# Gated linear attention with a maxout layer: a new order of the first loads, other due times in the planner, and two copies moved between engines

## The chip, the cores and the metric

The kernel runs on one core of one Trainium2 chip. The metric is the device time of one execution in microseconds (us). The core has five engines with a queue each: TensorE (PE), VectorE (DVE), ScalarE (ACT), GpSimd (POOL) and SyncE (SP), which here only issues loads. Each engine runs its instructions in the order of its program and waits at an instruction until what it needs is there.

## The reference: what is computed

```python
# q, k, v, alpha: (4 batches, 8 heads, 768 tokens, 48)
for t in range(S):
    state = alpha[:, :, t, :, None] * state + einsum('bhd,bhe->bhde', k[:, :, t], v[:, :, t])
    y[:, :, t] = einsum('bhd,bhde->bhe', q[:, :, t], state)
x = y.transpose(0, 2, 1, 3).reshape(3072, 384)
h1 = x @ w1                      # 384 x 1024
h2 = x @ w2                      # 384 x 1024
out = maximum(h1, h2) @ w_out    # 1024 x 384
```

## The kernel before

**Algebra.** The maxout is rewritten: max(h1, h2) = relu(x (w1 - w2)) + x w2. So the kernel forms `w12` = w1 - w2 (DVE, L447) and `w2o` = w2 w_out, and each output is relu(x w12) w_out + x w2o. The recurrence is done in chunks of 128 tokens: the logarithms of alpha are summed along the chunk, k is divided and q multiplied by the exponentials of the sums, and inside a chunk everything is a matmul.

**Units.** The 24 chunks go in pairs, so there are 12 units u = 0 to 11; unit u is batch u % 4 and token range u // 4. For a unit `gla(u)` makes: the logarithm of alpha on ACT (L468), the sums on PE (L490 for units 0 to 2, L479 after), the exponentials on ACT (`em` L517, in place in PSUM L519, `de` L522), `kn` on POOL (L560), `qn` on DVE (L562), their transposes on PE (L570) and the copy out of PSUM on DVE (`qu` L573 for units 0 to 2, `qk` L578 after), k by v on PE (`kv`, L589 or L632), the state `tm` (DVE L644; for the first chunk of a batch a plain copy, on ACT at L646 while u < TM_ACT, else on DVE at L648) and the scaled state `sb` on POOL (L619), q by k on PE (L661), the masked copy `pt` of it on DVE (four of them in a unit, L683), y on PE (L692, L695), and x transposed: `yc` on ACT (L703), PE L709, `xt` on DVE (L714 or L718). Then `moe(u)`: four groups `hp` on PE (L749, six matmuls each) with a relu into `gt` on ACT (L760) or DVE (L757), and the output sums on PE (L780: three matmuls with `w2o`, eight with `wo16`), a copy on ACT (L788) and the store.

**Weights.** w2 comes in three blocks of 512 KB (here w20, w21, w22), w_out in four of 384 KB (wo0 to wo3), w1 in four of 384 KB (w10 to w13). A w2 block goes through a cast on ACT (`w2h` L420), eight transposes on PE (L427), a copy out of PSUM (`w2T` L431, on ACT if its number is in WT_ACT, else on DVE) and eight matmuls with `wo16` (L437). `wo16` is the cast of w_out: block 0 on ACT, 1 to 3 on POOL (L452). Group g of `hp` needs `w12` group g, thus w1 block g and all three blocks of w2.

**Order.** Nothing is ordered by hand. Every step goes to a planner with `add`: engine, estimated duration, what it reads and writes, a key, and a `lat`, the time from its end to its result's being of use. `schedule` (L69) plays the steps in its own model of time: whenever an engine is free it takes, of the steps whose inputs have arrived in the model, the one with the smallest key. The instructions are then written in the order of the planned starts. So the planner's times set only the order; on the chip each engine waits for what is really late. Keys: 10 u plus a small number for `gla(u)`, 10 u + 20 (KEY_M) plus a small number for `moe(u)`, 3 (KEY_W) for the casts, transposes and copies of the weights, 11 (KEY_W12) for `w12`, 12 (KEY_WO) for the matmuls and copies of `w2o`. Eight PSUM banks are shared under CAPS.

**Loads.** All loads are issued by SP. The first 19 follow the list HEAD: a0 is alpha of unit 0, k1 is k of unit 1, and so on, each 384 KB for units 0 and 1. Their place on SP is fixed by the list. `load` and `load_w` give the planner their landing: SP's time for the issue plus a `lat` of 2.5 us (3.1 for w2), more for later units through LATE and LATER.

**Fillers.** Where the plan leaves PE idle in the first 40 us, matmuls on a constant are written in (L458); they produce nothing.

The lines that the change and the steps touch are in `load` (L382), `load_w` (L409), `w2_rows` (L419), `Plan.add` (L43, where PRI shifts a key) and the loop over HEAD (L816).

Of the kernel before, what the change touches and what calls it, by code (L numbers as in the profile page):

```python
# [23 lines left out]
class Plan:  # L24
# [18 lines left out]
    def add(self, eng, fn, dur, reads=(), writes=(), key=0.0, lat=None, ps=(), tiled=False, join=None):  # L43
        if writes:
            x = writes[0] if isinstance(writes[0], tuple) else writes
            d = self.pri.get(f"{eng}:{'.'.join(str(y) for y in x)}@{self.u}", 0)
            key, join = key + d, None if join is None else join + d
        o = Op(len(self.ops), eng, fn, dur, self.LAT[eng] + self.PAD if lat is None else lat, key)
        o.tiled, o.join = tiled, key if join is None else join
        for r in reads:  # L50
            if r in self.last_w:
                o.deps.add(self.last_w[r])
            self.readers.setdefault(r, []).append(o.n)
        for w in writes:
            if w in self.last_w:
                o.deps.add(self.last_w[w])
            for r in self.readers.pop(w, ()):
                if r != o.n:
                    o.deps.add(r)
            self.last_w[w] = o.n  # L60
        for x in (*reads, *writes, *ps):
            if x in self.psum and x not in o.ps:
                o.ps.append(x)
                self.psum[x][2] += 1
        o.w = (*writes, *reads)[:1]
        self.ops.append(o)
        return o
# [118 lines left out]

KEY_W12 = 11
KEY_W = 3
KEY_WO = 12
KEY_M = 20  # L190
CAPS = {'g': 6, 'm': 5, 'w': 3}
W12_POOL = ()
WT_ACT = ()
WO_ACT = (0,)
RELU_DVE = 1
TM_ACT = 1
X_LAST = 0
LATER = 0.6
LATE = 2.5
KEY_T2 = 17  # L200
TWO = (0, 1, 2)
# [7 lines left out]
PAIR_ON = 'POOL'  # L209
KN_DVE = ()  # L210
VX_DVE = ()
PRI = {}
HEAD = 'k0 a0 a1 q0 v0 k1 q1 w20 w22 w21 wo0 v1 wo1 wo2 wo3 w11 w10 w13 w12'


@with_exitstack
def kernel(
# [18 lines left out]
    nc = tc.nc  # L236
# [10 lines left out]
    def sbt(name, shape, dt, n=1):  # L247
        return [constp.tile(shape, dt, name=f"{name}{i}") for i in range(n)]
# [26 lines left out]
    w2h, = sbt("w2h", [128, ND, DFF], FP16)  # L275
    w12, = sbt("w12", [128, ND, DFF], FP16)
# [12 lines left out]
    def nat(t):  # L289
        return t.rearrange("p (a h d) -> p a h d", a=2, h=H)  # L290
# [4 lines left out]
    P = Plan()  # L295
    P.pri, P.u = PRI, None
    add = P.add
# [4 lines left out]
    def b32(x, n):  # L302
        return bank(x)[:, 0:n]
# [75 lines left out]
        add("DVE", lambda i=i: nc.vector.memset(SB[i], 0.0), 0.2, writes=[("sb", i)], key=-4)  # L379


    def load(u, what="akqv"):  # L382
        n, (b, cp) = u % NLD, (u % B, u // B)
        t0 = 256 * cp
        lat = 2.5 + max(0.0, min(LATE, LATE * (u - 1) / 3.0)) + LATER * max(0, u - 4)
        ws = [({4: "w2f", 5: "w1f", 6: "wof"}[u], g) for g in range(3 if u == 4 else 4)] if u in (4, 5, 6) else []

        def pairs(dst, src, keys):
            add("SP", lambda: nc.sync.dma_start(  # L389
                out=dst.rearrange("p (h x) -> p h x", h=H),  # L390
                in_=src[b, :, t0 : t0 + 256, :].rearrange("h (p r) d -> p h (r d)", r=2)),
                1.26 if u in TWO else 1.5, writes=[*keys, *ws], key=-1, lat=lat)

        if "a" in what:
            pairs(LD[n][:, 0, :], alpha, [("af", n)])
        rest = [x for x in (("k", "kf", KF, k), ("q", "qf", QF, q), ("v", "vf", VF, v)) if x[0] in what]
        if u in TWO:
            for _, nm, T, src in rest:
                pairs(T[n], src, [(nm, n, 0), (nm, n, 1)])
            return  # L400
        for a in range(2):
            for _, nm, T, src in rest:
                add("SP", lambda T=T, src=src, a=a: nc.sync.dma_start(
                    out=nat(T[n])[:, a],
                    in_=src[b, :, t0 + 128 * a : t0 + 128 * a + 128, :].rearrange("h p d -> p h d")),
                    0.99, writes=[(nm, n, a), *ws], key=-1, lat=lat)


    def load_w(m, g):  # L409
        fs = slice(256 * g, 256 * g + 256)  # L410
        if m == "2":
            dst, src, t = w2f[:, g, :], moe_w2[128 * g : 128 * g + 128, :], 1.36
        elif m == "1":
            dst, src, t = w1f[:, :, fs], moe_w1[:, fs].rearrange("(s p) f -> p s f", p=128), 1.15
        else:
            dst, src, t = wof[:, 2 * g : 2 * g + 2, :], moe_w_out[fs, :].rearrange("(s p) d -> p s d", p=128), 1.1
        add("SP", lambda: nc.sync.dma_start(out=dst, in_=src), t, writes=[(f"w{m}f", g)], key=-1, lat=3.1 if m == "2" else 2.5)

    def w2_rows(ds):  # L419
        add("ACT", lambda: nc.scalar.copy(out=w2h[:, ds, :], in_=w2f[:, ds, :]),  # L420
# [7 lines left out]
        add("PE", w_t, 0.445, reads=[("w2h", ds), "ident"], writes=[x], key=KEY_W)  # L428
        on = ds in WT_ACT
        cp = nc.scalar.copy if on else nc.vector.tensor_copy  # L430
# [5 lines left out]
        for f in range(NF):  # L436
            add("PE", lambda f=f: nc.tensor.matmul(  # L437
                b32(y, DM), lhsT=w2T[:, f, 128 * ds : 128 * ds + 128], rhs=wo16[:, f, :],
                start=(f == 0), stop=(f == NF - 1)),
                0.162, reads=[("w2T", ds), ("wo16", f // 2)], writes=[y], key=KEY_WO)  # L440
        add("ACT", lambda: nc.scalar.copy(out=w2o[:, ds, :], in_=b32(y, DM)),
            0.38, reads=[y], writes=[("w2o", ds)], key=KEY_WO)

# [81 lines left out]
    def gla(u):  # L525
# [69 lines left out]
        def chunk(a):  # L595
# [27 lines left out]
            if more:  # L623
# [14 lines left out]
                for h2 in range(2):  # L638
                    r, e = slice(64 * h2, 64 * h2 + 64), slice(D * h2, D * h2 + D)

                    def e_tm(r=r, e=e):
                        t = b32(kvp, DM).rearrange("p (j w) -> p j w", j=HP)
                        if has:
                            nc.vector.tensor_add(out=TM[tmi][r], in0=t[r, :, e], in1=sb[r, :, e])  # L644
                        elif u < TM_ACT:
                            nc.scalar.copy(out=TM[tmi][r], in_=t[r, :, e])  # L646
                        else:
                            nc.vector.tensor_copy(out=TM[tmi][r], in_=t[r, :, e])  # L648
                    on_act = not has and u < TM_ACT
                    add("ACT" if on_act else "DVE", e_tm, 0.32 if on_act else 0.37, reads=[kvp] + ([("sb", m4, h2)] if has else []),  # L650
# [162 lines left out]
    for ds in range(ND):  # L813
        P.ps(f"wq{ds}", 1, "w")
    add("SP", lambda: None, 0.6, key=-3)
    for x in HEAD.split():  # L816
        if x[0] == "w":
            load_w(x[1], int(x[2]))
        else:
            load(int(x[1]), x[0])  # L820
    gla(0)
    for g in range(4):
        weights(g)
# [2 lines left out]
    for u in range(NU):  # L826
        if u + 1 < NU:
            if f"a{u + 1}" not in HEAD:
                load(u + 1)
            gla(u + 1)  # L830
        moe(u)
# [38 lines left out]
```

## Time and profile before

| what | us |
|---|---|
| median of 5 runs | 138.8 (138.65 to 139.34) |
| the profiled execution, its own time | 138.8 |
| its span, first to last instruction | 137.1 |
| what lies around the span | 1.7 |
| PE busy, fillers (L458) among it | 130.6, of them 10.1 |
| DVE, ACT, POOL busy | 95.7, 81.8, 74.9 |
| first `hp` matmul of unit 0 starts | 25.38 |
| load queue of SP, share of the 16 DMA engines over the span | 71.7% |

The clock that PE was granted is full in all forty slices of the page. The page gives PE as 95% busy, but matmuls on the filler constant count as busy, so PE's row alone does not tell how much of the first 25 us is work; the table by stages and the filler rows do. A load's landing is its issue time plus the time to landing of its row. The times to the left in a timeline count from the start of the span.

### The profile page before, as it was taken

To read this page: it belongs to the slowest core of one execution; us is meant where nothing else is said; L and a number is where in the kernel's file an instruction comes from. 1 tells how busy PE (TensorE), PEld (TensorE's weight loads), DVE (VectorE), ACT (ScalarE), POOL (GpSimd) and SP (SyncE) were. 2 spreads that over 40 slices of the span, in tenths; PEclk is the share of its full clock that TensorE was granted. 3 is DMA by queue.
4 is the path that set the end of the run, shared out by engine and by line. 5 is a ranking of instruction groups with operands and counts; after the bars stand their busy time and mean duration, and the time that the engine had idled before them with its cause. 6 is when DMAs were issued, how large, how long until landed. Compare 5 with 4: busy or idle time off the path is not lost.

```text
span 137.1 us, 4253 instructions
## 1 busy us (share of the span) xinstructions
PE 130.6 (95%) x1671; PEld 101.4 (74%) x1671; DVE 95.7 (70%) x204; ACT 81.8 (60%) x174; POOL 74.9 (55%) x138
## 2 busy tenths in 40 slices
PE   6897999999999999999999999999999999999990
PEld 6776975777868777777877877777777778777870
DVE  4965999943799985966958859849839568583300
ACT  3394890879875765853944845837738548244440
POOL 7467549028596296574763972864757839200000
PEclk9999999999999999999999999999999999999999
DMA  4999999999997999979999999989978030030202
GB/s 98 324 325 402 374 374 352 289 251 254 260 268 153 271 223 195 299 149 213 286 183 306 230 223 260 236 176 271 258 140 225 5 115 2 5 115 0 105 29 100
DMA packets 84180, 28.59 MB, mean 209 GB/s; under 512 B 78400, under 2 KB 83392, under 8 KB 84160
## 3 DMA queue, kind: packets, MB, share of 16 engines
q1 hardware_dynamic: 81120, 23.60, 71.7%
q10 hardware_dynamic: 3040, 4.72, 9.1%
q8 instruction: 13, 0.21, 0.6%
q14 instruction: 7, 0.06, 0.1%
HBM read 23.59 MB, written 4.72 MB: 207 GB/s over the span
## 4 chain that ended last, share of the span: by engine, by line
PE 84%; DMA 5%; SPq 4%; DVE 3%; issue 1%; ACT 0%; ACTq 0%; DVEq 0%
PE pb L780 31%; PE pb L749 23%; PE pb L570 7%; DMA ld<-in_q_dram 5%; PE pb L661 4%; SPq L389 4%; PE pb L695 4%; PE pb L709 3%; PE pb L692 3%; PE pb L437 2%; PE pb L479 2%; PE pb L632 2%; DVE w2T L431 1%; PE pb L512 1%; PE pb L589 1%; DVE pt L683 1%
## 5 line engine op out<-in xcount | busy, mean ns | idle before, releaser
L780 PE MATMUL pb<-wo,gt 128*128 128x384 f16 (+2 forms) x200 | 39.5, 319 | 0.0
L560 POOL TENSOR_TENSOR kn<-ld,em 128x384 f16<-128x384 f32 x24 | 23.6, 997 | 23.8 <-ACT em L517 22.6
L749 PE MATMUL pb<-xt,w 128*128 128x256 f16 x288 | 35.7, 272 | 0.0
L683 DVE TENSOR_TENSOR pt<-pb,u 128x512 f16<-128x512 f32 x48 | 30.0, 683 | 0.4
L749 PEld LDWEIGHTS <-w 128*128 128x128 f16 x288 | 26.7, 98 | 3.4 <-DVE w L447 0.2
L760 ACT ACTIVATE gt<-pb 128x512 f16<-128x512 f32 x37 | 21.9, 608 | 9.5 <-PE pb L749 9.3
L619 POOL TENSOR_TENSOR sb<-tm,dd 64x192 f16<-64x192 f32 x40 | 20.1, 502 | 8.2 <-DVE tm L644 5.2
L788 ACT COPY os<-pb 128x384 f32<-128x384 f32 (+2 forms) x25 | 11.6, 466 | 19.0 <-PE pb L780 16.6
L780 PEld LDWEIGHTS <-gt 128*128 128x128 f16 x200 | 17.2, 97 | 7.6
L578 DVE COPY qk<-pb 128x1024 f16<-128x1024 f16 x18 | 12.3, 687 | 12.0 <-PE pb L570 8.8
L562 DVE TENSOR_TENSOR qn<-ld,pb 128x384 f16<-128x384 f32 x24 | 12.5, 550 | 6.5 <-ACT pb L519 4.6
L517 ACT ACTIVATE em<-pb 128x384 f32<-128x384 f32 x24 | 10.8, 488 | 8.6 <-PE pb L479 8.0
L780 PE MATMUL pb<-w2o,xt 128*128 128x384 f16 (+2 forms) x75 | 15.8, 320 | 0.0
L703 ACT CAST yc<-pb 128x384 f16<-128x384 f32 x24 | 11.8, 496 | 4.5 <-PE pb L695 4.4
L504 POOL TENSOR_TENSOR ls<-lg 128x384 f16<-128x384 f16 x10 | 9.1, 906 | 6.9 <-ACT lg L468 6.5
L468 ACT ACTIVATE lg<-ld 128x768 f16<-128x768 f32 x12 | 10.1, 846 | 3.7 <-DMA ld<-in_alpha_dram 3.7
L644 DVE TENSOR_TENSOR tm<-pb,sb 64x192 f32<-64x192 f32 x32 | 11.2, 352 | 0.6
L458 PE MATMUL pb<-wsrc 128*128 128x128 f16 x124 | 10.1, 244 | 1.1 <-DVE wsrc L310 1.1
L695 PEld LDWEIGHTS <-pt 128*128 128x128 f16 x192 | 9.7, 96 | 1.6 <-DVE pt L683 0.2
L718 DVE COPY xt<-pb 128x384 f16<-128x384 f16 x18 | 6.3, 352 | 6.5 <-PE pb L709 5.0
L757 DVE TENSOR_SCALAR gt<-pb 128x512 f16<-128x512 f32 x11 | 7.6, 692 | 4.6 <-PE pb L749 4.3
L519 ACT ACTIVATE pb<-pb 128x384 f32<-128x384 f32 x24 | 10.8, 482 | 0.0
(82 smaller groups left out, 195.3 us busy)
## 6 DMA issues: line engine op xcount, KB each, us to landing
ld<-in_alpha_dram SPq DMA_DIRECT2D x12, 384.0 KB, 5.2
out_dram<-os ACTq DMA_DIRECT2D x11, 384.0 KB, 3.8
ld<-in_k_dram SPq DMA_DIRECT2D x18, 192.0 KB, 4.5
ld<-in_q_dram SPq DMA_DIRECT2D x18, 192.0 KB, 4.6
ld<-in_v_dram SPq DMA_DIRECT2D x18, 192.0 KB, 4.7
ld<-in_moe_w_dram SPq DMA_DIRECT2D x3, 512.0 KB, 6.5
ld<-in_moe_w_out_dram SPq DMA_DIRECT2D x4, 384.0 KB, 7.6
ld<-in_moe_w_dram SPq DMA_DIRECT2D x4, 384.0 KB, 7.8
```

The lines of the kernel that those rows point to most:

```text
L560: add(on, lambda: ns.tensor_mul(out=kn[:, :, 0:D], in0=kin, in1=EM[m3]), 0.55 if on == "DVE" else 0.97, reads=[*rk, ("em", m3)], writes=[( ...
L562: add("DVE", lambda: nc.vector.tensor_mul(out=qn[:, :, 0:D], in0=qin, in1=csv(u, i)), 0.5, reads=[*rq, ("cs", u, i)], writes=[("qn", m3)], ...
L578: add("DVE", lambda: nc.vector.tensor_copy(out=QK[m3], in_=b16(tp, 1024).rearrange("p (w j c) -> p w j c", w=2, j=HP)), 0.6, reads=[tp], w ...
L619: add("POOL", lambda r=r, e=e: nc.gpsimd.tensor_mul(out=sb[r, :, e], in0=TM[tmo][r], in1=dd[r, :].unsqueeze(2).to_broadcast([64, HP, D])), ...
L644: nc.vector.tensor_add(out=TM[tmi][r], in0=t[r, :, e], in1=sb[r, :, e])
L683: add("DVE", lambda e=e: nc.vector.tensor_mul(out=pt[:, e], in0=b32(pp[e], 512).rearrange("p (j c) -> p j c", j=HP), in1=uv.unsqueeze(1).t ...
L695: nc.tensor.matmul(t[:, 96 * j + D * e : 96 * j + D * e + D], lhsT=pt[:, e, j, :], rhs=vc[:, 2 * j + e, :], start=not has, stop=(e == 1) o ...
L703: add("ACT", lambda: nc.scalar.copy(out=yc, in_=b32(yp, DM)), 0.38, reads=[yp], writes=[("yc", ci % 2)], key=kk)
L749: nc.tensor.matmul(t[:, m, :], lhsT=w12[:, ds, f * 128 : f * 128 + 128], rhs=xt[:, ds].rearrange("p a c -> p (a c)"), start=(ds == 0), sto ...
L760: add("ACT", lambda g2=g2, v2=v2: nc.scalar.activation(out=g2, in_=v2(), func=ACTF.Relu), 0.48, reads=[x], writes=[("gt", u % 3, f2)], key ...
L780: nc.tensor.matmul(b32(x, c1 - c0), lhsT=l, rhs=r, start=first and y == 0, stop=last and y == len(ws) - 1)
L788: add("ACT", lambda m=m, x=x, c0=c0, c1=c1: nc.scalar.copy(out=os_[:, m, c0:c1], in_=b32(x, c1 - c0)), 0.06 + w / 1200.0, reads=[x], write ...
```

## The change

The list of first loads is laid anew. a0 goes ahead of k0, v1 goes from after wo0 to before the first w2 block, q1 goes behind a w2 block, the three w2 blocks have other loads between them (before they were next to one another), and w1's blocks come as 2, 3, 0, 1 in place of 1, 0, 3, 2. In the planner a load that stands just in front of a w2 block now counts as landing 0.85 us later, one just behind a w2 block 0.3 us later. The copy `w2T` of block 0 goes from DVE to ACT (WT_ACT), and so do the two plain copies `tm` of unit 1 (TM_ACT). The matmuls and copies of `w2o` get key 16 in place of 12. LATER, by which the planner counts loads of unit 5 and on later, goes from 0.6 to 0.75 us a unit. And eleven single steps get their keys shifted by PRI: the name is engine, first tile written and unit, so `DVE:pt.0.0@1` is the first masked copy of unit 1's second chunk.

```diff
-KEY_WO = 12
+KEY_WO = 16
...
-WT_ACT = ()
+WT_ACT = (0,)
...
-TM_ACT = 1
+TM_ACT = 2
...
-LATER = 0.6
+LATER = 0.75
...
-PRI = {}
-HEAD = 'k0 a0 a1 q0 v0 k1 q1 w20 w22 w21 wo0 v1 wo1 wo2 wo3 w11 w10 w13 w12'
+PRI = {'PE:hp.1.2@1': 3, 'PE:hp.2.3@2': -5, 'ACT:w2h.2@0': -9, 'DVE:pt.1.0@5': 10, 'DVE:pt.0.0@3': 9, 'PE:hp.1.0@1': 3, 'PE:kv.5.1@5': 7.5, 'PE:tp.3.1@3': 3, 'DVE:pt.0.0@1': 9, 'PE:hp.2.2@2': 8, 'DVE:qn.2@4': -5}
+HEAD = 'a0 k0 a1 q0 k1 v0 v1 w22 q1 w21 wo0 w20 wo1 wo2 wo3 w12 w13 w10 w11'
...
-    def load(u, what="akqv"):
+    def load(u, what="akqv", more=0.0):
...
-        lat = 2.5 + max(0.0, min(LATE, LATE * (u - 1) / 3.0)) + LATER * max(0, u - 4)
+        lat = 2.5 + max(0.0, min(LATE, LATE * (u - 1) / 3.0)) + LATER * max(0, u - 4) + more
...
-    def load_w(m, g):
+    def load_w(m, g, more=0.0):
...
-        add("SP", lambda: nc.sync.dma_start(out=dst, in_=src), t, writes=[(f"w{m}f", g)], key=-1, lat=3.1 if m == "2" else 2.5)
+        add("SP", lambda: nc.sync.dma_start(out=dst, in_=src), t, writes=[(f"w{m}f", g)], key=-1, lat=(3.1 if m == "2" else 2.5) + more)
...
-    for x in HEAD.split():
+    head = HEAD.split()
+    for i, x in enumerate(head):
+        after = i + 1 < len(head) and head[i + 1][:2] == "w2" and x[:2] != "w2"
+        before = i > 0 and head[i - 1][:2] == "w2" and x[:2] != "w2"
+        more = 0.85 if after else 0.3 if before else 0.0
         if x[0] == "w":
-            load_w(x[1], int(x[2]))
+            load_w(x[1], int(x[2]), more)
         else:
-            load(int(x[1]), x[0])
+            load(int(x[1]), x[0], more)
```

## The prediction

> **What bounds the kernel now.** I read the busy table by stretches first, then the same table for the fillers (L458) alone, then the chain of waits, then the rows around the first `hp`, then the load rows.
>
> Columns of the first fence: stretch, its length, then busy us and instructions of PE, weight loads, DVE, ACT, POOL, then clock, DMA share, GB/s.
>
> ```profile
> 6.00:12.80 6.80, 6.10 (x102) 5.11 (x101) 4.19 (x12) 5.33 (x14) 4.76 (x7) 1.00 1.14 351
> 12.80:21.40 8.60, 7.30 (x131) 5.95 (x131) 8.37 (x17) 6.17 (x10) 4.34 (x7) 1.00 1.07 377
> 21.40:25.40 4.00, 3.98 (x55) 2.74 (x56) 3.94 (x8) 1.21 (x4) 2.69 (x5) 1.00 1.11 343
> 25.40:133.90 108.50, 108.50 (x1338) 82.99 (x1334) 75.35 (x149) 66.95 (x146) 59.16 (x104) 1.00 0.79 186
> ```
>
> The same stretches, fillers alone:
>
> ```profile
> 6.00:12.80 6.80, 3.05 (x46) 2.63 (x46) 1.00 1.14 351
> 12.80:21.40 8.60, 2.32 (x27) 1.68 (x27) 1.00 1.07 377
> 21.40:25.40 4.00, 0.00 (x0) 0.00 (x0) 1.00 1.11 343
> ```
>
> PE has no gap from 21.4 to the end and runs at full clock, so there only the amount of work counts, and the change does not alter it. Time can be won or lost in what PE does not use before. That is all of 0 to 6; from 6 to 12.8 it is 6.80 - 6.10 + 3.05 = 3.75; from 12.8 to 21.4 it is 8.60 - 7.30 + 2.32 = 3.6. In the last of these DVE is busy 8.37 of 8.60: PE waits for DVE. The chain of waits says where that begins (start, length, what):
>
> ```profile
> 6.51 6.32 DMA ld<-in_q_dram
> ...
> 12.96 0.57 DVE qn L562
> ...
> 17.15 0.67 DVE w2T L431
> ...
> 18.49 0.69 DVE qu L573
> 19.18 1.20 DVE w2T L431 x2
> 20.41 0.69 DVE pt L683
> ```
>
> q1 is issued at 6.51 and lands at 12.83; then comes a nearly closed row of DVE work, with three `w2T` copies in it. The wait at the head of it is this (waiter, releaser: us, times, longest):
>
> ```profile
> DVE qn L562 <- DMA ld<-in_q_dram: 1.5, 1, 1.5
> ```
>
> In these 1.5 us the q by k of unit 0 was ready (L661 began at 11.97), and its four `pt` stood behind `qn` of unit 1 in DVE's order until 13.89. At the far end of the stage (start, length, engine, line):
>
> ```profile
> 23.24 0.69 DVE L683 TENSOR_TENSOR pt<-pb,u 128x512 f16<-128x512 f32 x1
> 23.85 1.13 DVE L447 TENSOR_TENSOR w<-ld,ld 128x768 f16<-128x768 f32 x1
> ```
>
> The first w1 block lands at 15.34 + 7.88 = 23.22, but its subtraction begins only at 23.85, behind a `pt`, and the first `hp` at 25.38.
>
> **The loads.** From the issue rows and their times to landing, the small loads land one after another 1.2 us apart (4.12, 5.33, 6.51, 7.74, 8.95, 10.17), w2 blocks 1.28 apart, w_out blocks 1.07, w1 blocks 1.13. One step is out of line: q1, 2.66 after k1. Laid anew with the same steps, the seventh taking the 2.66 again: a0 4.1 (was 5.33), k0 5.3, a1 6.5, q0 7.7 (the same), k1 8.95, v0 10.2, v1 12.8 (was 18.9), w22 14.1, q1 15.3 (was 12.8), w21 16.6, wo0 17.7, w20 19.0 (w2 was complete at 16.7), wo1 20.0, wo2 21.0, wo3 22.1, w12 23.2, then 24.4, 25.5, 26.6. From wo1 on nothing moves, since the same bytes stand in front.
>
> Is the seventh late because of w2 behind it? In the table of loads from 10 to 13 us there is this row (packets, MB, share of 16 engines):
>
> ```profile
> q8 instruction: 1, 0.02, 1.9%
> ```
>
> 1.9% of 16 engines' 3 us is 0.9 us of one DMA engine, in the middle of q1. So I take the lateness to hang on the time, not on w2; it will be v1's. The other end is that every load in front of a separate w2 block is late by 2.66 - 1.21 = 1.45 us. The Trainium skill (Runtime: NRT & Kernel Launch, Instruction fetch mechanics) speaks for that other end: it calls instruction blocks of 16 KiB "mostly hidden". By that rule w2 would be to blame and the total about 141.1 instead of my 138.2; no other run shows it yet.
>
> **The change part by part.**
>
> 1. *a0 first.* Its logarithm can start 1.2 us earlier (5.42 to about 4.2). q0 keeps its landing at 7.74, so `qn` of unit 0 moves only from 8.61 to about 7.85. Up to 0.75 us for unit 0, none of it on the end by itself: it serves item 2.
> 2. *q1 later, unit 0 ahead of it.* `qn` of unit 1 starts 15.3 - 12.83 = 2.5 later. In its place DVE does the four `pt` of unit 0 (2.48 us in the timeline) before q1, where it stood idle for 1.5. So unit 0 ends about 2.5 earlier and unit 1 starts 2.5 later with the `pt` out of its way. About nothing; if DVE's order were left as it is, it would cost the 2.5.
> 3. *`w2T` of block 0 and two `tm` copies to ACT.* DVE loses 0.67 + 0.73 = 1.4 us between 15 and 24. ACT gets two `tm` at 0.31 (row L646) and one copy of 1024 columns from PSUM, which no row shows: between 1.02 (row L788: 0.27 for 128 columns, 0.107 for each further 128) and 1.22 (twice the relu of 512, 0.61). I take 1.05, as the cast of 1024 columns (L420). ACT is busy 6.17 of 8.60 and then 1.21 of 4.00, so this lies beside other work. Left on DVE after q1: two `qn` 1.1, two `qu` 1.4, four `pt` 2.7, one `w2T` 0.67, two `xt` 0.7: 6.6 us from 15.3, with room before 23.2.
> 4. *w2 complete only at 19.0.* Block 0: cast 1.05, transposes 0.45, copy 1.05, waits between them some 0.4: 22.0, then eight `w2o` matmuls at 0.16. The cast of wo3 (landed 22.1, 0.82 on POOL) ends at 23.0 and holds the last six anyway, so all of `w2o` can be done at about 24.0. At nothing, with 1 us of cover.
> 5. *First `hp`.* Subtraction from 23.2 to 24.2 or 24.35 (rows of 0.95 and 1.13), `hp` at about 24.4 instead of 25.38: 1.0 us earlier. This is the floor of the stage; unit 2's loads land from 27.6 on, so there is no other work for PE.
> 6. *What is not done by then.* Before, at 25.38, only the transposes of unit 1 were open (0.34). With PRI the last `pt` of unit 1 goes behind the subtractions, so y of its second chunk (0.37) stays open too and is paid later. 1.0 - 0.37 = 0.6 us won. Between 0.2 (some 0.4 of `w2o` also open) and 1.35 (all of it done, transposes too).
> 7. *KEY_WO, hp.1.x, hp.2.x.* `w2o` may fill PE between the four `hp` groups, whose w1 blocks come 1.13 apart while a group takes 0.66. There is y, `w2o`, and the output sums of unit 0 to fill with; at nothing, between -0.3 and, were the three pauses of 0.47 left empty, +1.4.
> 8. *LATER and the other PRI.* Loads from unit 3 on land 1.2 to 13 us before their first use, so a due time 0.15 us a unit later only reorders. The shifted `pt`, `tp`, `kv` and `qn` stand where DVE is busy 7 to 9 of 10 us and PE always has other work queued; at nothing. Without that cover, one `pt` waited for in full: +0.7; a gain is excluded because PE has no gap there.
>
> Sum, against the profiled execution: its own 138.8 (span 137.1 and 1.7 around it) less 0.6 gives 138.2. The median of the runs is 138.8 as well, so no shift.
>
> **The rivals.**
>
> *All of it comes in* (137.5). Everything that does not need w1 is done when `hp` starts: 138.8 - 1.35. For it: DVE's 6.6 us in 7.9. Against it: the `pt` set behind the subtractions.
>
> *It moves and does not gain* (138.8). DVE is still closed when the first w1 block lands, or y and `w2o` of about 1 us are left over, and the start of `hp` a microsecond earlier is paid back. For it: before, too, PE was closed already from 21.4, four microseconds before `hp`.
>
> *Slower: w2 delays whatever stands in front of it* (139.7). Then it is not the time but w2, and separating its blocks makes three late steps out of one. One additional step of 1.45 moves all later loads: 138.2 + 1.45 = 139.65; two give 141.1. It decides from the point where the first w1 block lands after 24.2, for then the 1.0 of item 5 is gone. Against it: around the same step the queue moved 377 GB/s instead of 351, so nothing stood still. For it: only one instance is in the trace.
>
> **How the numbers follow.** Forecast 0.44, all of it 0.20, no gain 0.18, slower 0.18. A difference within 0.3% (138.4 to 139.2) is about what a measurement of this kernel cannot tell from none. Of the forecast's case 0.02 ends inside it (its lower end of 0.2 won), so faster is 0.42 + 0.20 = 0.62, same 0.18 + 0.02 = 0.20, slower 0.18. The range runs from 137.3 (all of it, and 0.2 of item 7) to 139.7 (one late step); it leaves out two late steps and a shift of the w1 blocks to earlier.
>
> **What would show it.** Right: first logarithm at about 4.2; no wait of DVE on q1 that has `pt` of unit 0 behind it; one `w2T` of L431 on ACT at 1.0 to 1.2 us; first w1 block landed at about 23.2, first `hp` at 24.4, fillers and idle before 24.4 about 0.6 less than the 13.35 before 25.4 here. Wrong: a q1 after 16.5 or a w1 block after 24.2 (w2 is to blame), PE rows with idle between 24 and 30 (item 7), or a stage after 40 us in which PE is below 10.00 of 10 (item 8).

## The result, and the profile after

The changed kernel takes 138.48 us (138.26 to 139.12, 32 runs); the kernel before takes 138.76 (138.54 to 139.57, 54 runs). The ratio is 0.998, interval 0.9973 to 0.9987: faster by 0.28 us, where 0.6 was forecast. The profiled executions took 138.48 and 138.8, their spans 136.8 and 137.1. So the sign is as forecast, the size is not, and the question is which step promised the rest.

The busy table by stretches, after (columns as in the prediction):

```profile
6.00:12.80 6.80, 6.80 (x117) 5.86 (x115) 5.56 (x13) 4.95 (x12) 4.09 (x6) 1.00 1.14 338
12.80:21.40 8.60, 8.60 (x170) 7.39 (x168) 7.82 (x17) 7.39 (x15) 6.03 (x10) 1.00 1.06 385
21.40:25.40 4.00, 4.00 (x47) 2.73 (x45) 3.52 (x6) 2.43 (x5) 1.94 (x3) 1.00 1.11 342
25.40:133.60 108.20, 108.20 (x1329) 82.77 (x1327) 74.90 (x148) 66.80 (x145) 59.22 (x104) 1.00 0.79 187
```

The same for the fillers (L458) alone:

```profile
6.00:12.80 6.80, 3.84 (x62) 3.54 (x63) 1.00 1.14 338
12.80:21.40 8.60, 3.84 (x51) 2.80 (x48) 1.00 1.06 385
21.40:25.40 4.00, 0.00 (x0) 0.00 (x0) 1.00 1.11 342
```

PE now looks closed from 6 us on, but by fillers: from 6 to 21.4 they take 7.68 us, where before there were 5.37 of fillers and 2.00 of idle. Over the whole head, 0 to 25.4, PE's busy time after is:

```profile
0.00:25.40 25.40, 24.35 (x368) 1.00 1.01 321
```

and the fillers in it:

```profile
0.00:25.40 25.40, 12.02 (x148) 10.42 (x148) 1.00 1.01 321
```

Unused are 25.40 - 24.35 + 12.02 = 13.07; before it was 25.40 - 22.08 + 10.07 = 13.39. By these rows the head holds 0.3 us more work than before, about the whole gain. Busy time covers short waits, as the ends of matmuls are modelled, so the account below, from starts alone, is the better measure; it gives 0.23 for the head. After 25.4 PE is closed in both kernels.

The w1 end of the head, DVE, after (start, length, engine, line; in brackets idle time and who ended it):

```profile
22.37 0.67 DVE L683 TENSOR_TENSOR pt<-pb,u 128x512 f16<-128x512 f32 x1
23.46 0.96 DVE L447 TENSOR_TENSOR w<-ld,ld 128x768 f16<-128x768 f32 x1 [0.41 <-DMA ld<-in_moe_w_dram]
```

DVE is through with its `pt` and waits 0.41 for the w1 block, landed at 23.33; the subtraction ends at 24.42. So far this is the forecast (23.2 and 24.2 to 24.35). PE after:

```profile
24.91 0.33 PE L709 MATMUL pb<-ident,yc 128*128 128x128 f16 x3
25.07 0.65 PE L437 MATMUL pb<-wo,w2T 128*128 128x384 f16 x3
25.56 2.13 PE L749 MATMUL pb<-xt,w 128*128 128x256 f16 x18
```

The first `hp` starts at 25.56 and not at 24.4: `w2o` (L437) and the transposes (L709) stand in front of it. It is even 0.18 later than before (25.38), in the faster kernel. It then runs three groups without a pause, where before two ran from 25.38.

The loads after (row: load, size, us to landing):

```profile
ld<-in_v_dram SPq DMA_DIRECT2D x1, 384.0 KB, 5.0
ld<-in_moe_w_dram SPq DMA_DIRECT2D x1, 512.0 KB, 6.5
```

and the queue row from the table of loads from 10 to 13 us, after (packets, MB, share of 16 engines):

```profile
q8 instruction: 1, 0.02, 1.8%
```

v1, the load in front of w22, is issued at 6.64 and lands at 11.59, 1.31 after v0: in time. w22, issued at 7.83, lands at 14.31, 2.72 later, and the instruction packet lies in its time, at 11.05. So the late step hangs neither on what stands in front of w2 nor on being the seventh. The other landings are within 0.25 us of those laid out in the prediction (q1 15.43, w21 16.72, w20 19.06, first w1 block 23.33).

**Two accounts used below.** *PE's account:* every interval from one matmul's start to the next, counted as work up to the shortest interval its kind shows (56 ns for 128 columns, 109 for 256, 162 for 384), the rest of it as waiting; fillers apart.

| PE, us | before | after | e8 |
|---|---|---|---|
| work | 115.8 | 115.8 | 115.8 |
| of it done by 25.4 us | 11.87 | 12.10 | 12.75 |
| fillers | 10.0 | 11.0 | 9.0 |
| waits and half speed | 6.9 | 5.5 | 6.7 |
| PE's last end | 133.91 | 133.61 | 132.81 |

Fillers stand where the planner itself sees nothing to do; waits are what the chip adds to the plan. The change buys 1.34 us of waits off with 1.03 of planned idle time.

*Planned and real:* the planner's own model gives every step a time. "Slip" is the real start of an `hp` group less its planned start.

| | planned end of PE | slip at first `hp` | slip at the end | median |
|---|---|---|---|---|
| before | 132.91 | 0.49 (24.89, 25.38) | 0.84 | 138.76 |
| after | 133.19 | 0.07 (25.49, 25.56) | 0.26 | 138.48 |

The changed order is 0.28 longer by the planner's model, and the chip falls 0.58 less behind it: -0.30, as measured. This is bookkeeping, since planned end and slip add up to the real end by definition; where the slip comes from has to be read in the traces. Both accounts are of one profiled execution of each kernel.

### The profile page after: what moved, and what is told of

Its sections match the earlier page's. It is cut to its first block, busy times and chain, and to the rows that moved or that the text cites. A ratio compares the mean times of both kernels' runs of the same rounds, so it can differ in the third digit from the quotient of the medians.

```text
span 136.8 us, 4306 instructions
## 1 busy us (share of the span) xinstructions
PE 132.6 (97%) x1695; PEld 103.3 (76%) x1695; DVE 95.7 (70%) x201; ACT 84.0 (61%) x177; POOL 75.2 (55%) x138
## 4 chain that ended last, share of the span: by engine, by line
PE 96%; ACT 0%; ACTq 0%; issue 0%; DVE 0%
PE pb L780 31%; PE pb L749 23%; PE pb L570 8%; PE pb L458 8%; PE pb L661 5%; PE pb L695 3%; PE pb L709 3%; PE pb L437 3%; PE pb L692 3%; PE pb L479 2%; PE pb L490 2%; PE pb L632 2%; PE pb L512 1%; PE pb L427 1%; PE pb L589 1%; ACT os L788 0%
## 5 line engine op out<-in xcount | busy, mean ns | idle before, releaser
L458 PE MATMUL pb<-wsrc 128*128 128x128 f16 x148 | 12.0, 245 | 1.1 <-DVE wsrc L310 1.1
L458 PEld LDWEIGHTS <-wsrc 128*128 128x128 f16 x148 | 10.4, 112 | 1.3 <-DVE wsrc L310 1.0
```

What stands on the lines that cost most here:

```text
L458: nc.tensor.matmul(PB[b][:, 0:128], lhsT=wsrc, rhs=wsrc, start=True, stop=True)
```

## The experiments

All ratios are to the kernel before, run in the same series, with their intervals. Its median was 138.76 beside the changed kernel, 138.82 beside e1 to e4, 138.73 beside e5 to e8 and 138.91 beside e9 to e11; so a difference in us between medians of two series carries up to 0.2 us that is not the kernel's. Theory A throughout: a kernel's time is the planned end of its order plus some 5.2 us, as long as the due times are honest (after: 138.48 - 133.19 = 5.29), and more where the plan counts on what comes late (before: 5.85). The rivals are in each expectation.

### e1: before, q1 counted late

```diff
-        lat = 2.5 + ... + LATER * max(0, u - 4)
+        lat = 2.5 + ... + LATER * max(0, u - 4) + (0.9 if what == "q" and u == 1 else 0.0)
```

> The kernel before with one number changed: the planner counts q1 0.9 us later, which is when it lands in the trace of before (planned 11.92, landed 12.83). Theory A (the time is the length of the laid order plus the slip of the chip behind it): the order laid with this truth is 1.1 us longer by the planner's own account (its last PE step ends at 134.02 instead of 132.91), and the chip's slip behind it shrinks from 0.6 to 0.1 at the first hp groups, so 138.76 + 1.1 - 0.5 = 139.3. Rival B (a true due time is by itself what makes the change faster): 138.76 - 0.5 = 138.2. Rival C (the first hp hangs on the first w1 block, as the prediction had it): the first hp is not earlier than 25.3, so 138.7.

Measured: 139.22, ratio 1.002 (0.9997 to 1.0043). The slip falls to 0.30 at the first `hp` and 0.13 at the end (0.49 and 0.84 before), and the planned end rises to 134.02: the median lies 5.2 above it, as A has it. Honesty about one load alone gains nothing here, because the order laid with it is 1.11 longer.

### e2: after, `w2o` last

```diff
-KEY_WO = 16
+KEY_WO = 24
```

> The kernel after with KEY_WO 24 in place of 16, so that the first hp groups go ahead of the rest of the w2o matmuls. The planner then starts hp at 24.19 instead of 25.49, and its last PE step ends 0.21 later (133.40 instead of 133.19). Rival C (the start of hp, held by the first w1 block, sets the end): hp 1.2 us earlier, 137.3. Theory A: what counts is only how much of PE's time before it closes is fillers and waits, so hp at about 24.5 and still 138.5 to 138.7.

Measured: 138.93, ratio 0.9995 (0.9973 to 1.0017). This does what step 5 of the prediction wanted. PE in e2:

```profile
24.56 0.83 PE L749 MATMUL pb<-xt,w 128*128 128x256 f16 x6
...
25.40 0.81 PE L437 MATMUL pb<-wo,w2T 128*128 128x384 f16 x4
26.05 0.82 PE L749 MATMUL pb<-xt,w 128*128 128x256 f16 x6
...
27.52 0.49 PE L437 MATMUL pb<-wo,w2T 128*128 128x384 f16 x2
27.85 0.22 PE L458 MATMUL pb<-wsrc 128*128 128x128 f16 x1
```

`hp` starts at 24.56, 1.0 earlier than in the changed kernel, `w2o` fills between the groups as step 7 had it, and the kernel is not faster: by the medians it is 0.45 slower than the changed kernel (A had 138.5 to 138.7), though the interval of its ratio still reaches the changed kernel's 0.998. The start of `hp` is no floor and no measure: what is put off is paid behind it, and a filler at 27.85 shows the plan running out of work. The slip at the first `hp` is 0.37, of which 0.27 is there from 22.26 on, where `w2o` waits 0.3 for a cast of w_out on POOL; the first w1 block lands only at 23.43.

### e3 and e4: the shifted keys and the moved copies taken back

```diff
-PRI = {'PE:hp.1.2@1': 3, ...}
+PRI = {}
```

> The kernel after with PRI empty, so all keys as before but KEY_WO. The planner's last PE step ends at 134.02 instead of 133.19. Theory A: 138.48 + 0.8 = 139.3, with more idle or filler time of PE. The prediction's items 7 and 8 (the shifted keys are worth about nothing): 138.5, at most 0.3 away.

Measured: 139.12, ratio 1.002 (0.9999 to 1.004). The eleven shifted keys, "at nothing" in steps 7 and 8, are worth 139.12 - 138.48 = 0.64 by the medians (against the kernel before beside it, 138.82, e3 is 0.30 slower); the planned end without them is 134.02, 0.83 later.

```diff
-WT_ACT = (0,)
+WT_ACT = ()
...
-TM_ACT = 2
+TM_ACT = 1
```

> The kernel after with WT_ACT empty and TM_ACT 1: the w2T copy of block 0 and the two plain tm copies of unit 1 go back to DVE. The planner's last PE step ends at 133.56 instead of 133.19. Theory A: 138.48 + 0.4 = 138.85. The prediction's item 3 (1.4 us of DVE in a stage that DVE bounds): 139.2 to 139.9. If DVE is no bound at all in the changed order: 138.5.

Measured: 138.81, ratio 0.9996 (0.9972 to 1.002). The copies on ACT are worth 0.33 by the medians (planned: 133.56 - 133.19 = 0.37), with an interval that still contains 0.998. They take 1.4 us off DVE, and about a quarter of that arrives.

### e5, e6 and e7: fillers

e5 leaves up to eight matmuls out of each run of fillers but the first; e6 leaves all but the first run out; e7 is e5 with a correction of a constant (DVE, L326, two instructions) moved from 7 to 29 us.

```diff
-        n = max(0, int((gap - 0.85) / 0.107 if t < 1.0 else (gap - 0.1) / 0.056))
+        n = max(0, int((gap - 0.85) / 0.107 if t < 1.0 else (gap - 0.1) / 0.056 - 8))
```

> The kernel after with up to 8 matmuls fewer in each row of fillers behind the first (109 become 56), no order changed. If fillers hold real work back (in the trace of after the q by k of unit 0 waits 0.4 us behind fillers and the kv of unit 0 about 1.2): 138.48 - 0.2 to - 0.4, so 138.1 to 138.3. If the work behind a row of fillers waits for loads and DVE anyway: 138.4 to 138.5.

Measured: 138.69, ratio 1.0002 (0.9983 to 1.0021). The first `hp` starts 0.26 earlier than after, with a slip of -0.19; from 34.6 us on the slip is +0.72. The waits from 28 to 36 us of e5 say what came between (waiter, releaser: us, times, longest):

```profile
POOL vx L543 <- DMA ld<-in_v_dram: 1.6, 1, 1.6
...
ACT vx L547 <- DMA ld<-in_v_dram: 0.8, 1, 0.8
```

v2 lands at 33.23 (31.31 after). Fewer instructions on PE shift the places at which its program is fetched, and one packet now falls at 31.08, into v2. Filler counts can move later loads. The profiled execution of e5 took 139.13, 0.44 above the median, so this delay need not be in every execution; the median is above both expectations.

e6, with no fillers after the first run:

```diff
-        n = max(0, int((gap - 0.85) / 0.107 if t < 1.0 else (gap - 0.1) / 0.056))
+        n = max(0, int((gap - 0.85) / 0.107 if t < 1.0 else 0))
```

> The kernel after without any filler behind the first row of 39. Two questions. The clock: in the trace of after a 384-column matmul took 320 ns at 5.8 us and 162 from 7 us on; if PE falls back to half speed in the pauses, then matmuls before 20 us take twice as long and the total is 139 to 140; if not, as with the short rows, 138.1 to 138.5. The late load: PE has 218 instructions fewer behind it at 14 us, so its first instruction block (packet of 16384 bytes) comes later than the 9.8 to 11.05 of the runs so far. If that packet makes the late load, v1 (in front of w22) lands 1.2 us behind v0 and a later load is 1.4 late; if w2 makes it, v1 lands 2.6 behind v0 as in most runs.

Measured: 139.76, ratio 1.0077 (1.0046 to 1.0108). The stretches of e6:

```profile
6.00:12.80 6.80, 3.91 (x44) 3.04 (x43) 5.07 (x12) 4.23 (x10) 3.84 (x5) 0.75 1.14 342
12.80:21.40 8.60, 6.37 (x116) 5.40 (x113) 6.86 (x13) 7.39 (x15) 6.30 (x10) 0.80 1.07 386
```

and its PE row after the longest pause:

```profile
9.36 0.61 PE L570 MATMUL pb<-ident,qn 128*128 128x128 f16 x4 [2.89 <-DVE qn L562]
```

The granted clock falls to 0.75 and 0.80 in the two stretches, the four transposes take 0.61 (0.40 in the changed kernel), and the slip is 1.33. The fillers earn their place; how many stand at a gap's end is another matter.

```diff
-    todo = [(P.ops[i].start, i, P.ops[i].fn) for i in order]
+    todo = [(29.0 if P.ops[i].eng == "DVE" and P.ops[i].w == ("t2",) else P.ops[i].start, i, P.ops[i].fn) for i in order]
```

> The kernel after with short fillers as in the run with up to 8 matmuls fewer, and the correction of t2 (two DVE instructions, 1.54 us from 7.25 in the trace of after, 0.58 in that of before) moved on DVE behind the w12 subtractions. qn of unit 0 then starts at about 7.95 instead of 8.82, and unit 0 is 0.9 earlier up to its pt. If the early part counts for the end: 0.5 to 0.9 below the run with short fillers. If q1 (landed at 15.4) sets what follows, as theory A has it: the same as that run within 0.1, and DVE idles longer before qn of unit 1.

Measured: 138.53, ratio 0.999 (0.9979 to 1.0001). DVE in e7:

```profile
7.85 1.02 DVE L562 TENSOR_TENSOR qn<-ld,pb 128x384 f16<-128x384 f32 x2 [0.64 <-DMA ld<-in_q_dram]
...
15.35 1.02 DVE L562 TENSOR_TENSOR qn<-ld,pb 128x384 f16<-128x384 f32 x2 [1.72 <-DMA ld<-in_q_dram]
```

`qn` of unit 0 now starts at 7.85, as step 1 had it (8.82 after), and DVE gives the time back at once: it waits 1.72 for q1. What unit 0 gains ahead of q1 shows no gain at the end, since q1 lands at 15.23. Against e5 there are 0.16 us, which lie within the two intervals; here the third packet falls at 29.96, into a3, which nobody waits for.

### e10: before, the packet moved off q1

Two runs of fillers are shortened, so that PE's program is fetched later; the order is that of before.

```diff
         n = max(0, int((gap - 0.85) / 0.107 if t < 1.0 else (gap - 0.1) / 0.056))
+        n = {5: 0, 17: 5}.get(n, n) if 7.0 < t < 9.0 else n
```

> The kernel before, same order, same due times, with 17 fillers fewer (5 and 12 of the second and third row, in which PE waits for loads and exponentials of unit 1 anyway). That moves PE's first instruction block behind: it came at 10.58 while q1 was moving; 34 PE instructions later is about 11.3 to 11.8, while the first w2 block moves. If the packet makes q1 late: q1 lands at 11.4 to 11.6 instead of 12.83, the slip of 0.63 at the first hp groups falls to about 0.1, and the old order with its optimistic due times beats the changed kernel: 138.2 to 138.3. If w2 behind q1 makes it late: q1 at 12.8 and 138.7. Open risk: the third packet comes about 1 us later too, among the loads of k and q of unit 2, and may cost what the first one gave.

Measured: 138.94, ratio 0.9995 (0.9977 to 1.0014), above both expectations. The packet falls at 13.12, into w22, which lands 2.27 after the block in front of it; q1 lands at 11.96 (12.83 before), still 1.68 after k1. DVE in e10:

```profile
12.09 1.02 DVE L562 TENSOR_TENSOR qn<-ld,pb 128x384 f16<-128x384 f32 x2 [0.54 <-DMA ld<-in_q_dram]
...
22.38 0.69 DVE L683 TENSOR_TENSOR pt<-pb,u 128x512 f16<-128x512 f32 x1
23.91 1.24 DVE L447 TENSOR_TENSOR w<-ld,ld 128x768 f16<-128x768 f32 x1 [0.84 <-DMA ld<-in_moe_w_dram]
```

and the waits of PE from 20 to 27 us:

```profile
PE pb L437 <- POOL wo L452: 0.4, 1, 0.4
PE pb L749 <- DVE w L447: 0.2, 1, 0.2
```

DVE's row is 0.87 us earlier up to the last `pt`. PE follows it: k by v of unit 0 starts at 12.70 (13.57 before), and the `w2o` matmul planned at 19.43 starts at 19.37, where it was 0.54 late before. So q1 in time does take that slip away. But nothing is won, because two other late things take its place: at 21.80 `w2o` waits for a cast of w_out on POOL (the slip is 0.41 from there to the first `hp`, at 25.30), and the second `hp` group waits for w1, planned at 22.81 and landed at 23.38, since w22 was late instead (slip 0.80 behind it, 0.63 before).

### e8, e9 and e11: a new order with measured due times

e8 gives each of the first loads the landing that a trace shows for its place, not the rule of 0.85 and 0.3, and takes the list, keys and copies with which the planner's end is earliest.

```diff
-KEY_W12 = 11
+KEY_W12 = 25
-KEY_M = 20
+KEY_M = 18
-WO_ACT = (0,)
-RELU_DVE = 1
+WO_ACT = (1,)
+RELU_DVE = 3
-KN_DVE = ()
+KN_DVE = (0,)
-PRI = {'PE:hp.1.2@1': 3, ...}
-HEAD = 'a0 k0 a1 q0 k1 v0 v1 w22 q1 w21 wo0 w20 wo1 wo2 wo3 w12 w13 w10 w11'
+PRI = {'PE:op.0.1.0@0': 10, 'PE:hp.2.3@2': 8, 'PE:pp.2.1.0@2': -5, 'PE:op.1.0.0@1': 3, 'PE:kv.3.1@3': 5, 'PE:kv.3.0@3': 5, 'PE:pp.0.0.0@0': 3}
+HEAD = 'a0 a1 q0 k0 v0 q1 w22 k1 w21 v1 w20 wo0 wo1 wo2 w10 wo3 w13 w12 w11'
...
-        more = 0.85 if after else 0.3 if before else 0.0
+        more = {'a0': 0.0, 'a1': 0.0, 'q0': 0.0, 'k0': 0.0, 'v0': 0.0, 'q1': 0.0, 'w22': 0.43, 'k1': 0.98, 'w21': 0.31, 'v1': 0.85, 'w20': 0.18, 'wo0': 0.75, 'wo1': 0.72, 'wo2': 0.69, 'w10': 0.67, 'wo3': 0.64, 'w13': 0.61, 'w12': 0.59, 'w11': 0.56}.get(x, 0.0)
```

> The kernel after with an order laid on the landings that the traces show: q1 goes sixth, in front of all of w2 (HEAD a0 a1 q0 k0 v0 q1 w22 k1 w21 v1 w20 wo0 wo1 wo2 w10 wo3 w13 w12 w11), every load's due time is its place in the measured sequence with 1.45 for the seventh, and seven keys and four choices of engine or key are others. The planner's last PE step ends at 132.84 instead of 133.19. Theory A (length of the order plus a slip near 0.1): 138.1, with fewer fillers before 20 us. If the planner's account says nothing on differences of 0.3: anywhere from 138.3 to 139.2.

Measured: 137.82 (137.60 to 138.46, 6 runs), ratio 0.9936 (0.992 to 0.9953): it beats both kernels. The first stretches of e8:

```profile
6.00:12.80 6.80, 6.20 (x123) 5.37 (x119) 6.45 (x16) 5.26 (x15) 3.48 (x6) 1.00 1.14 353
12.80:21.40 8.60, 7.36 (x138) 6.06 (x136) 8.47 (x18) 7.14 (x12) 6.52 (x10) 1.00 1.07 376
```

and the fillers in them:

```profile
6.00:12.80 6.80, 3.38 (x49) 2.84 (x49) 1.00 1.14 353
12.80:21.40 8.60, 2.39 (x22) 1.48 (x22) 1.00 1.07 376
```

The fillers are 1.91 less than after. PE shows idle again instead (0.60 and 1.24), and the account says what that leaves: fillers 2.0 less, waits 1.2 more, 0.65 more work done by 25.4. DVE is busy 6.45 and 8.47 in these stretches (5.56 and 7.82 after): the order has more for it to do early. The planned end is 132.84, 0.35 earlier than after, and the slip is -0.40 at the first `hp` and -0.19 at the end: the chip runs ahead of the plan. So 137.82 lies 4.98 above the planned end, 0.28 below what A gave. e8 changes the list, the due times, the keys and four choices at once; which of them carries the gain is not separated.

e9 is e8 with the shortened fillers of e5:

> The new order with up to 8 matmuls fewer in each row of fillers behind the first (85 become 21). The run with short fillers on the kernel after had its first hp 0.26 earlier and lost 0.8 at v of unit 2, on whose way its third instruction packet came. If the packet does not meet a load that is waited for: 137.82 - 0.2, so 137.6; if it does: 138.2 to 138.6.

Measured: 137.91 (137.78 to 138.29, 6 runs), ratio 0.9923 (0.9903 to 0.9944). No difference from e8 that these runs could tell.

e11 is the changed kernel with only e8's list and its due times:

> The kernel after with nothing but the load list and the due times of the new order (q1 sixth, before all of w2). The planner's last PE step ends at 133.46, 0.27 above the kernel after and 0.62 above the new order. Theory A: 138.5 to 138.75, though q1 lands 5 us earlier. If the place of q1 by itself made the new order faster: 137.8 to 138.0.

Measured: 138.83, ratio 0.9989 (0.9962 to 1.0016), with a planned end of 133.46. The list of the best order, with its due times, is no better by itself: the keys found for one list did not serve the other.

## Why the prediction was wrong in size

**The step that failed is step 5**, "`hp` at about 24.4 instead of 25.38: 1.0 us earlier. This is the floor of the stage". The load and the subtraction came as said (23.33, 24.42), but PE was closed until 25.56, with `w2o` that step 4 had done at 24.0, and y and transposes that step 6 put behind `hp`. And the start of `hp` measures nothing while PE is closed in front of it: e2 starts `hp` 1.0 earlier and is no faster (0.45 slower by the medians). I had the reason in hand, a PE without a gap from 21.4, and wrote it down under the rival that does not gain. What counts is the work done by then, 0.23 more, and the waits behind it (0.62 from 25.4 to 40, 0.77 before).

Step 6's 0.37 is void with step 5. The others:

- *The loads:* right. v1 was in time in front of w2 and the packet's own load late, so the rival that w2 delays whatever stands in front of it falls; e6 shows three loads in front of w2 blocks in time (v1, q1, wo0, each 1.05 to 1.20 after the one before) and w20 late by the packet at 16.23. Wrong was only that the lateness stays in seventh place.
- *Step 1:* the logarithm starts at 4.33 (4.2 said). `qn` of unit 0 starts at 8.82, not 7.85, since DVE's correction of a constant took 1.54 us in place of 0.58; e7 shows no cost of this at the end.
- *Step 2:* right in kind. The first `pt` of unit 0 starts at 12.38 (13.89 before), not at 11.4; fillers still ran when its q by k could have begun at 11.55 (it began at 11.95).
- *Step 3:* right in its duration (`w2T` on ACT 1.01 us, 1.05 said). Its worth was left inside step 5; e4 gives 0.33 by the medians.
- *Step 4:* w2 complete at 19.06 and copied by 22.25 (19.0 and 22.0 said), but `w2o` was not done at 24.0. With key 16 it gives way to y and ends at 25.56.
- *Step 7:* no pause between the `hp` groups, as said. *Step 8* is wrong by size: e3 gives 0.64 for the shifted keys that the two steps counted at nothing. A key's shift has no duration to read off a row; its price is what the whole order becomes.

**The rivals.** "It moves and does not gain" was nearest in its mechanism, with 0.28 between it and the result: y and `w2o` are indeed left over, only in front of `hp`. "All of it comes in" falls with step 5.

**What stands in its place.** The old order waits on q1, as the chain of waits in the prediction had it: q1 is planned at 11.92 and lands at 12.83. PE runs 0.44 ahead of the plan at the end of the q by k of unit 0 (planned 12.64, real 12.20) and is 0.71 behind it at the next step (12.85, 13.57), before which it stands still. Two of its rows before:

```profile
13.57 0.52 PE L589 MATMUL pb<-vx,kn 64*128 64x96 f16 x16 [0.98 <-DVE qn L562]
...
21.87 3.10 PE L437 MATMUL pb<-wo,w2T 128*128 128x384 f16 x18
```

Fillers give part of it back, two short waits (0.22 at 19.24, 0.31 at 21.42) add to it, and from 21.87 PE's rows follow one another without a gap up to the first `hp`, with a slip of 0.49 from 22.04 on. So the 0.49 at the first `hp` is made before the first w1 block lands (23.22); w1 adds only the step from 0.49 to 0.63 at the second `hp` group. e10 agrees: with q1 in time the slip is gone up to 20.2 us. In the changed kernel the trace shows no wait of PE, fillers aside, from 12 us to the first `hp`: q1 (planned 14.84, landed 15.43) and w1 (22.81, 23.33) are late there too, but the order has work or planned idle time in front of them. By the account above this lowers the slip by 0.58 and makes the plan 0.28 longer. Taking single parts back (e2, e3, e4) costs 0.33 to 0.64 by the medians, more than the whole change gains, though only e3 lies clear of the changed kernel by the intervals: the parts fit one another and don't add up.

**What stays open.** How much of the 0.28 is q1's was not measured. e1 counts q1 right and its slip falls, but it is another order, 1.11 longer; e10 brings q1 in time and meets other waits; and no kernel here has the new list without its later due times. And A is coarse: its constant lies between 4.98 and 5.53 over e1, e2, e3, e4, e8 and e11, a spread twice the gain of the change. A came within 0.2 us for e1, e3, e4 and e11, and was off by more for e2, e8 and e10. That it fits the 0.28 to 0.02 is partly luck.

## What to carry to other kernels

Where the bottleneck engine has no gap for microseconds ahead of a milestone, an earlier milestone is worth nothing by itself: add up what that engine leaves unused, idle and filled alike, over the whole head. In a kernel that a planner has ordered, price an edit by two terms, the length of the new plan and how far the chip falls behind it; the second is read as planned against real start at many points, and followed back to the last idle time of the engine, for a slip that is read at a milestone need not be made there. Late due times pay only where the plan has other work for the wait.

## What the runs showed of the hardware

**A fetch of program is a load that others wait for.** One 16 KB packet on the instruction queue takes 0.9 to 1.1 us on one DMA engine. In each of the thirteen traces the first of them goes with one late load, the first or second to land behind the packet's start: it lands 2.3 to 3.0 us after the one before it, where 1.1 to 1.3 is the normal step. Six of them:

| kernel | packet at | load that is late, its step |
|---|---|---|
| before | 10.58 | q1, 2.66 |
| after | 11.05 | w22, 2.72 |
| e2 | 9.78 | v1, 2.58 |
| e10 | 13.12 | w22, 2.27 |
| e9 | 13.65 | w21, 2.99 |
| e6 | 16.23 | w20, 2.61 |

Moving the packet by fillers (e6, e10) moved the late step with it. Behind it everything stays some 1.4 us late as long as the queue is full, so the first w1 block lands at 23.1 to 23.4 in the nine kernels that have the same bytes in front of it and no other late step. Not every packet does this: the second one, at 20.02 before (1.10 us long) and 19.34 after (1.11), delays nothing, the loads behind it land 1.0 to 1.1 apart. What decides is not shown. The Trainium skill (Runtime: NRT & Kernel Launch, Instruction fetch mechanics) calls the crossing of such a block "mostly hidden". For PE, which shows no wait on it here, that agrees; for the load beside it, these runs show 1.0 to 1.7 us. The place of the packet goes with PE's instruction count: the third one comes when PE has started 702 to 746 matmuls and weight loads, in all thirteen traces, so adding or dropping a dozen matmuls can move the delay to another load (e5: v2, 0.8 us of ACT's time). The count fixes it only roughly: e5 and e7 have the same matmuls in the same order, and the first packet at 12.58 and 10.82.

**Short pauses halve PE's clock.** In e6 the longest pause between 6 and 21 us is 2.89 us and the next 1.61, and the granted clock is 0.75 and 0.80 there. Divided where the clock changes, the same time reads (stretch, length, PE busy, clock, DMA share, GB/s):

```profile
5.75:9.16 3.41, 0.71 (x11) 1.00 1.17 325
9.16:12.58 3.42, 3.22 (x28) 0.50 1.12 359
12.58:15.99 3.41, 1.60 (x46) 1.00 1.09 404
15.99:19.40 3.41, 3.00 (x37) 0.50 1.04 381
```

Each half-speed stretch is 3.4 us long and follows one of the same length in which PE was busy 0.71 and 1.60 us. The Trainium skill (TensorE: Matmul & The Clock Gate, Part 1: The HAM clock gate) puts the fall at an idle window of about 3.4 us; with these rows the measurement decides, and pauses below that are enough.

**A neighbour holds up a small DVE instruction.** The two corrections (32x512, L326) take 0.28 each when POOL is idle, and 0.53 and 1.00 in the changed kernel, where POOL's `kn` (6.64 to 8.63) runs beside them. Moving a load ahead by 1.2 us brought the two together. e5 has both cases in one trace: 1.07 beside a `kn`, then 0.28 with POOL idle. In the thirteen traces nine of the corrections are stretched, all of them beside a `kn`, and each ends 0.14 to 0.16 us after a `kn` ends, as if it were held until then; two more, in e2 and e3, start with a `kn` and take 0.28. No run kept everything else and moved `kn` alone.
